# A two-layer convolution and MLP network with its gradients on one core: layer 1's forward in a fixed order on PE, and loads, stores and a normalisation moved within their queues

## The chip, the core and the metric

The kernel runs on one core of a Trainium2 chip. The metric is the device time of one execution in microseconds (us). Engines are named as in the profile: PE multiplies matrices (PEld is its weight load), DVE is the vector engine, ACT the scalar (activation) engine, POOL the general one, and SP issues most of the DMAs. [...]

## What is computed

The reference runs a forward pass of four blocks on 2048 tokens of 448 features, and returns its output together with the gradients of all inputs:

```python
x = A_q
x = x + A(layernorm(x), k, v, shift_k, ssm_k, ssm_D)   # q * (long convolution of kv + kv * D)
x = x + B(layernorm(x), w1, w2)                        # silu(x @ w1) @ w2, 448 -> 1792 -> 448
x = x + A(layernorm(x), k, v, shift_k, ssm_k, ssm_D)
x = x + B(layernorm(x), w1, w2)
out, vjp = jax.vjp(f, A_q, A_k, A_v, A_shift_k, A_ssm_k, A_ssm_D, B_w1, B_w2)
return (out, *vjp(grad_out))
```

Within A, k is convolved with a kernel of four taps (shift_k) and multiplied by v to give kv; kv is convolved along the sequence with ssm_k, by Fourier transforms of length 4096 in the reference; the result multiplies the layer's normalised input. The convolution's output Y doesn't depend on x, so both layers share it.

## The kernel before

**The prefix (`_ssm_prefix`).** It computes Y by a two-stage Fourier transform written as matmuls: `conv` makes kv from k by four-tap matmuls, `stage1_kv` and `_fft_stage1` the first stage, `turn` transposes on PE, `_fft_stage2` the second stage. The spectrum K of ssm_k stands in the tile Z (as Ka), and KB holds K with its halves swapped, which takes DMAs from SBUF to SBUF (`_swap_halves_dma`, shown as KB<-Z, issued by POOL). A loop of eight rounds (h, i) runs conv for kv, the first stage of the round before, the turns of K (first half) and the second stage of K (second half). In rounds 2 and 3 it also does the first layer normalisation of token group 0 (`_ln`, lines 425 and 426; tile na0, input x0c0), pinned in its place among DVE's and ACT's instructions. `cons_ka` copies K's chunks out of PSUM and stores them to DRAM (spec_K, line 413), and `cons_prod` does the same with the spectrum of kv (spec_KV, line 448), then multiplies it by Ka and by KB (pa, pb) for the inverse transform. Both kinds of store are issued by POOL, and so share its queue with the swaps. The weights w1sb and w2sb are asked for after the call of the prefix (lines 185 to 189), on SP.

**The layers (`Main`).** Tokens run in four chunks of 512 (c), each of four tiles of 128. `first` makes X, the normalised input and its transpose nT for chunk 0. `a_fwd` is block A for one chunk: normalisation, product with Y, sum into X. `b_pre` is block B's normalisation, `b_tr` the transposition to nT (`transp`: 2 x 8 transpositions on PE into ps_t, and two copies to nT). `h(c, L, nT, half, hold)` computes half of the 1792 hidden features in four groups of one or two tiles of 128: matmuls into ps_h (line 537, tag mm, two buffers), the silu to aT on ACT (L629), and a copy dT of the input to silu (L113), which the gradient needs. That copy is made by DVE, except for the third group of half 0, whose copy is ACT's. `out` multiplies aT by w2sb (ps_o, line 658, tag po with two buffers) and adds it to X on DVE (L659).

The 448 features of nT are three full blocks of 128 and one of 64 rows. `contract` orders a group's matmuls: `at` other than 0 puts the whole ones first and the half ones (64 rows) last, `at` 0 the other way round. [...]

In the first loop of `run`, chunk c of layer 1 does h for half 1, b_tr for chunk c+1, h for its half 0, and then `out` for chunk c. The order on each engine is the framework's choice from its own costs, with the order of the program as priority. The second loop does layer 2's forward together with layer 2's backward (`ga`: gradient of the hidden features, ps_g, ghp, ghT; `gn`: ps_n, line 740, and the backward of the normalisations), the third layer 1's backward with the weight gradients (`ps_d`, line 904) woven in.

**Spilled tiles.** aT and ghT are turned by DMA transposes (`store_turned`, L503; one buffer "turned") and stored to A_d and GH_d (L504) one step later by `flush`; the dT of layer 1 are stored to DT_d and loaded again (`load_d`, L769, tile dTl, tag D with three buffers). ACT turns dTl into silu's slope in place (`slope`, L614), in layer 1's backward in a hook after each tile's lb_u (L742). In `ga` the load for a later chunk and the turn of the present ghT come at the same step.

**The end (`_gw1`).** It computes the last weight gradient, feature tile by feature tile: two loads of 512 KB (dstat<-GH_d, L902, and dstat<-GP_d, L900, a DMA transpose), 32 matmuls, a copy dout on ACT; `turn` turns dout by a DMA transpose to do (L941), and `store` stores the tile turned before (L933, L934). These DMAs are all SP's.

Of the kernel before, what the change touches and what calls it, by code (L numbers as in the profile page):

```python
# [17 lines left out]
P = 128  # L18
S = 2048
D = 448  # L20
# [100 lines left out]
def kernel(  # L121
# [60 lines left out]
    k.yk = ctx.enter_context(tc.tile_pool(name="yk", bufs=1, side="right", reuse_waits="tile"))  # L182
    k.Ysb = k.yk.tile([P, J, D], BF16, name="Ysb", tag="Y")
    _ssm_prefix(k)
    k.w1sb = k.wk.tile([P, ND, F], BF16, name="w1sb", tag="WA")
    nc.sync.dma_start(out=k.w1sb[:, 0:3, :], in_=k.B_w1[0:384].rearrange("(c p) f -> p c f", p=P))
    nc.sync.dma_start(out=k.w1sb[:, 3, :], in_=k.B_w1[320:448])
    k.w2sb = k.wk.tile([P, NF, D], BF16, name="w2sb", tag="WB")
    nc.sync.dma_start(out=k.w2sb[:], in_=k.B_w2.rearrange("(c p) d -> p c d", p=P))
    k.psum = ctx.enter_context(tc.tile_pool(name="psum", bufs=1, space=PSUM, reuse_waits="tile"))  # L190
    k.xg = ctx.enter_context(tc.tile_pool(name="xg", bufs=1, side="right", reuse_waits="tile"))
    k.Xp = k.xg.tile([P, NT, 512], BF16, name="X", tag="X")
# [94 lines left out]
def _ssm_prefix(k):  # L287
# [4 lines left out]
    with ExitStack() as es:  # L292
# [113 lines left out]
        def cons_ka(ci, ps):  # L406
            sl = slice(ci * 1024, (ci + 1) * 1024)
            _copy(nc, bal.pick(1024), Ka[:, sl], ps[:])
            if ci % 2 == 1:
                lo, hi = (ci - 1) * 1024, (ci + 1) * 1024  # L410
                if ci > 8:
                    _swap_halves_dma(k, KB, Ka, lo, hi, nc.gpsimd)
                nc.gpsimd.dma_start(out=k.SPEC_d["K"][:, lo:hi], in_=Ka[:, lo:hi])

        k.na0 = k.dp.tile([P, 4, D], BF16, name="na0", tag="dstat", bufs=3)
        prev = None
        for h in range(2):
            for i, jq in enumerate((1, 2, 3, 0)):
                kvt = conv(h, jq)
                if prev:  # L420
                    stage1_kv(*prev)
                prev = (h, jq, kvt)
                if h == 0:
                    turn(A1Kf, Z, (0, 1, 5, 6)[i])
                if 4 * h + i in (2, 3):
                    _ln(k, work, 0, lambda tl: k.x0c0[:, tl, :], 0, k.na0, ((2 * i - 4, 2 * i - 2),), pin=True, store=i == 3)
                if h == 1:
                    _fft_stage2(k, Z, psum, cons_ka, range(2 * i, 2 * i + 2))
        for i in range(4):
            _swap_halves_dma(k, KB, Ka, 2048 * i, 2048 * (i + 1), nc.gpsimd)  # L430
        stage1_kv(*prev)
        A1f = A1kv[:].rearrange("p a c n s -> p a (c n s)")
        for i in range(3):
            _fft_stage2(k, Z, psum, cons_ka, range(8 + 2 * i, 10 + 2 * i))
# [8 lines left out]
        def cons_prod(ci, ps):  # L443
            sl = slice(ci * 1024, (ci + 1) * 1024)
            xs = Zf[:, sl]
            _copy(nc, bal.pick(1024), xs, ps[:])
            if ci % 2 == 1:
                nc.gpsimd.dma_start(out=k.SPEC_d["KV"][:, (ci - 1) * 1024:(ci + 1) * 1024], in_=Zf[:, (ci - 1) * 1024:(ci + 1) * 1024])
            pa = work.tile([P, 1024], BF16, name="pa", tag="pa", bufs=4)
            pb = work.tile([P, 1024], BF16, name="pb", tag="pb", bufs=4)  # L450
            nc.vector.tensor_tensor(out=pa[:], in0=xs, in1=Ka[:, sl], op=ALU.mult)  # L451
            nc.vector.tensor_tensor(out=pb[:], in0=xs, in1=KB[:, sl], op=ALU.mult)  # L452
            bal.add("dve", 1.4)
            hold.append((pa, pb, ci))
            if len(hold) > 2:
                pa, pb, cj = hold.pop(0)
                _fft_inv_stage2_chunk(k, pa, pb, False, B1, cj, psum)
# [22 lines left out]
class Main:  # L480
# [58 lines left out]
    def transp(self, src, dst):  # L539
        nc, k = self.nc, self.k  # L540
        blocks = [(0, 128), (128, 256), (256, 384), (320, 448)]
        rows = P
        for h in range(2):
            pt = k.psum.tile([P, 2, 512], BF16, name="ps_t", tag="tr", bufs=2)
            for u in range(2):
                lo, hi = blocks[2 * h + u]
                for tl in range(4):
                    nc.tensor.transpose(pt[:rows, u, tl * P:(tl + 1) * P], src[:, tl, lo:hi], k.ident[:])
            _copy(nc, k.bal.pick(1024, dve_ns=0.53), dst[:rows, 2 * h:2 * h + 2, :], pt[:rows])

    def first(self):
# [24 lines left out]
                keep(nc.vector.tensor_scalar(out=n_g[:, tl, :], in0=X[:, tl, :], scalar1=r[:, tl:tl + 1], scalar2=nmr[:, tl:tl + 1], op0=ALU.mult, op1=ALU.add))  # L576
        nc.gpsimd.dma_start(out=_pm(k.N_d[1][:])[:, 0:4, :], in_=n_g[:])
        nT = self.ch.tile([P, ND, 512], BF16, name="nT", tag="nT", bufs=2)
        pts = [k.psum.tile([P, 2, 512], BF16, name="ps_t", tag="tr", bufs=2) for _ in range(2)]
        for tl in range(4):  # L580
            for b, lo in enumerate((0, 128, 256, 320)):
                nc.tensor.transpose(pts[b // 2][:, b % 2, tl * P:(tl + 1) * P], n_g[:, tl, lo:lo + P], k.ident[:])
        nc.scalar.copy(nT[:, 0:2, :], pts[0][:])
        self.held = keep(nc.vector.tensor_copy(nT[:, 2:4, :], pts[1][:])).ins
        return nT
# [28 lines left out]
            self.k.last_slope = self.nc.scalar.activation(s, s, ACT.Derivative_silu)  # L614
            self.k.bal.add("act", 0.5 * n)

    def h(self, c, L, nT, half, hold, pre=None):
        nc, k = self.nc, self.k
        aT = self.td.tile([P, NF // 2, 512], BF16, name="aT", tag="T", bufs=3)
        dT = self.td.tile([P, NF // 2, 512], BF16, name="dT", tag="D", bufs=3)  # L620
        hold.append((aT, dT))
        d0 = pre() if pre else None
        for ft0, n, at in ((0, 2, 1), (2, 2, 0), (4, 2, 1), (6, 1, 1)) if half == 0 else ((7, 1, 1), (8, 2, 1), (10, 2, 0), (12, 2, 1)):
            ps = k.psum.tile([P, 2, 512], FP32, name="ps_h", tag="mm", bufs=2)
            self.contract(ps, self.w1sb, nT, ft0, n, at)
            o = ft0 - 7 * half
            a = aT[:, o:o + n, :]
            tm = dT[:, o:o + n, :]
            last = nc.scalar.activation(a, ps[:, 0:n, :], ACT.Silu)  # L629
            e = nc.scalar if o == 4 or (o, c, L, half) == (0, 0, 0, 0) else nc.vector  # L630
            _copy(nc, e, tm, ps[:, 0:n, :])
            k.bal.add("act", 0.52 * n)
            k.bal.add(*(("act", 0.52 * n) if e is nc.scalar else ("dve", 0.6 * n)))
        if L == 1:
            if half == 1:
                with self.tc.issue_after(last.ins):
# [10 lines left out]
                self.next_piece()  # L647
        if L == 1:
            self.store_turned(k.A_d[1], aT, c, half)
        return d0  # L650

    def out(self, c, aT, last):
        nc, k, X = self.nc, self.k, self.X
        for tl in range(4):
            t = 4 * c + tl
            po = k.psum.tile([P, 512], FP32, name="ps_o", tag="tr" if last and tl % 2 else "po", bufs=2)
            for ft in range(NF):
                nc.tensor.matmul(po[:, :D], lhsT=aT[ft // 7][0][:, ft % 7, tl * P:(tl + 1) * P], rhs=self.w2sb[:, ft, :], start=(ft == 0), stop=(ft == NF - 1))  # L658
            nc.vector.tensor_tensor(out=X[:, t, :], in0=X[:, t, :], in1=po[:, :D], op=ALU.add)  # L659
            k.bal.add("dve", 0.62)  # L660
        if last:
            nc.gpsimd.dma_start(out=_pm(k.outs[0][0])[:, 4 * c:4 * c + 4, :], in_=X[:, 4 * c:4 * c + 4, :])

    def g_load(self, c):
        gb = self.ch.tile([P, 4, 512], BF16, name="gb", tag="gb", bufs=2)
# [14 lines left out]
    def ga(self, c, L, gT, dT, mid=None, loads=(None, None)):  # L680
# [3 lines left out]
        for fp in range(NF // 2):  # L684
# [15 lines left out]
            if fp in (3, 6):  # L700
                hh = (fp - 3) // 3
                if loads[hh]:
                    ld.append(self.load_d(*loads[hh]))
                if L == 1 or hh == 0:
                    self.store_turned(k.GH_d[L], ghT[hh], c, hh)
                else:
                    self.flush()
                    self.store_plain(nc.sync, k.GP_d, ghT[hh], c, 0)
# [77 lines left out]
    def run(self):  # L786
# [6 lines left out]
        def hook(d):  # L793
# [2 lines left out]
                    self.slope(d, (tl,))  # L796
            return run

        self.h(0, 0, nT, 0, cur)
        for c in range(4):  # L800
            if c < 3:
                with self.tc.issue_after(self.held):
                    self.a_fwd(c + 1, 0, xs[c])
                nb = self.b_pre(c + 1, 1)
            else:
                gb = self.g_load(0)
                na, nb = self.a_fwd(0, 2, None), self.b_pre(0, 3)
            self.h(c, 0, nT, 1, cur)
            nT = self.b_tr(nb)
            fol = []  # L810
            self.h((c + 1) % 4, 0 if c < 3 else 1, nT, 0, fol)
            if c == 3:
                gT = self.g_turn(gb[:])
            self.out(c, cur, False)
            cur = fol
        for c in range(4):
            d0 = self.h(c, 1, nT, 1, cur, (lambda: self.load_d(0, 0)) if c == 3 else None)
            if c < 3:
                na1 = self.a_fwd(c + 1, 2, None)
            self.out(c, cur, True)  # L820
            if c < 3:
                gb_next = self.g_load(c + 1)
            if c == 3:
                with self.tc.issue_after(k.last_slope.ins):
                    self.slope(d0)
            box = []
            if c < 3:
                ghT = self.ga(c, 1, gT, cur, lambda fp: box.append(self.b_pre(c + 1, 3)) if fp == 2 else None)
# [14 lines left out]
            na, nb = na1, nb1  # L843
            if c < 3:
                gb = gb_next
        k.jobs = _gw2(k, k.dp, range(3), [(k.dp, "dstat", 3)], first=k.go_jobs.ins)
        bb = nc.cur_bb.bb

# [73 lines left out]
def _gw1(k, pool, slots):  # L922
# [13 lines left out]

    def turn(ft, o):
        if ft < NF - 2:
            store()
            o7 = pool.tile([P, ND, P], BF16, name="do7", tag="do7", bufs=2)  # L940
            nc.sync.dma_start_transpose(out=o7[:], in_=o[:])  # L941
            turned.append((ft, o7))
            return
        store()
# [278 lines left out]
```

## Time and profile before

| What | us |
|---|---|
| Median of three runs (737.02 to 741.23) | 739.4 |
| The profiled execution | 738.77 |
| Its span, from first to last instruction | 736.6 |
| Prefix and start of the layers, to the first ps_h | 0 to 102.5 |
| Layer 1's forward, to the first group of layer 2's chunk 0, half 1 | 102.5 to 211.6 |
| Layer 2's forward and backward | 211.6 to about 410 |
| Layer 1's backward | about 410 to 519.6 |
| Suffix (convolution's gradient, weight gradients) | 519.6 to 736.6 |
| PE busy 690.3, DVE 507.6, ACT 424.1, POOL 62.7 | share of span 94%, 69%, 58%, 9% |
| DMA: 180.11 MB, 245 GB/s as a mean | |

The busy time of PE is the union of its matmuls' times with modelled ends[...]. The stages overlap at their edges. In the window view each row is a stretch of the span with the busy time of each engine in it, the granted clock of PE and the mean share of the DMA engines; in the timeline a gap before an instruction stands in brackets with what ended it.

### The profile page before, as it was taken

What the parts mean: (1) busy time and instruction counts of PE and PEld (TensorE: products, weight loads), DVE (VectorE), ACT (ScalarE), POOL (GpSimd) and SP (SyncE); (2) the same over time, 40 slices, a digit from 0 to 9 for tenths busy, and PEclk for the clock granted to TensorE, in tenths of its full rate; (3) what the DMA queues carried; (4) which work ended last, traced back from release to release, by engine and by line L of the source; (5) the groups of instructions that cost most, each with busy time, mean ns of one, the idle gap of its engine ahead of it and who ended that gap; (6) DMA issues with size and microseconds to landing.
All of it is one profiled execution on the core that took longest, in us unless ns stands there. A gap on an engine that the chain in (4) does not pass through costs nothing. (4 is left out here: it accounts for less than half of the span.)

```text
span 736.6 us, 12192 instructions
## 1 busy us (share of the span) xinstructions
PE 690.3 (94%) x4753; PEld 362.6 (49%) x4753; DVE 507.6 (69%) x1059; ACT 424.1 (58%) x539; POOL 62.7 (9%) x111
## 2 busy tenths in 40 slices
PE   6988789999999998999999799999999999999987
PEld 5766533443344443443444334445465767755533
DVE  4878888787743597895958788798224777199423
ACT  4688877766437577487576476763723666531101
POOL 1143221111100002000000000000000000000000
PEclk9999999999999999999999989999999999999999
DMA  9979969999875878979999999997799999899966
GB/s 311 240 179 277 354 212 319 280 290 281 244 153 143 202 158 208 188 205 200 239 223 289 185 348 263 255 270 257 268 252 215 297 322 348 279 275 243 208 144 154
DMA packets 234789, 180.11 MB, mean 245 GB/s; under 512 B 179178, under 2 KB 215598, under 8 KB 233580
## 3 DMA queue, kind: packets, MB, share of 16 engines
q1 hardware_dynamic: 228238, 156.34, 82.4%
q0 software_dynamic: 5872, 22.65, 9.0%
q8 instruction: 37, 0.61, 0.4%
q10 hardware_dynamic: 622, 0.35, 0.3%
q14 instruction: 20, 0.16, 0.1%
HBM read 69.58 MB, written 63.77 MB: 181 GB/s over the span
## 5 line engine op out<-in xcount | busy, mean ns | idle before, releaser
L904 PEld LDWEIGHTS <-dstat 128*128 128x128 bf16 x896 | 85.1, 98 | 80.8 <-DMA dstat<-GP_d 4.4
L537 PE MATMUL ps_h<-nT,w1sb 128*128 128x512 bf16 (+1 forms) x448 | 102.1, 381 | 6.8 <-DVE dT L113 5.2
L537 PE MATMUL ps_g<-gT,w2T 128*128 128x512 bf16 (+1 forms) x448 | 96.0, 381 | 3.2 <-ACT ghp L690 3.1
L740 PE MATMUL ps_n<-w1T,ghT 128*128 128x448 bf16 x448 | 92.6, 360 | 5.0 <-ACT lb_u L742 3.6
L904 PE MATMUL ps_d<-mov,dstat 128*128 128x448 bf16 x448 | 89.5, 352 | 3.5 <-DMA dstat<-GP_d 3.5
L629 ACT ACTIVATE aT<-ps_h 128x1024 bf16<-128x1024 f32 (+1 forms) x64 | 58.4, 916 | 55.2 <-PE ps_h L537 38.3
L658 PE MATMUL ps_o<-w2sb,aT 128*128 128x448 bf16 x448 | 90.1, 353 | 0.0
L113 DVE CAST dT<-ps_h 128x1024 bf16<-128x1024 f32 (+1 forms) x55 | 58.3, 1063 | 27.8 <-ACT aT L629 27.8
L537 PEld LDWEIGHTS <-w1sb 128*128 128x128 bf16 (+1 forms) x448 | 35.9, 96 | 69.7 <-issue 41.2
L740 PEld LDWEIGHTS <-ghT 128*128 128x128 bf16 x448 | 43.5, 99 | 48.6 <-issue 7.7
L537 PEld LDWEIGHTS <-w2T 128*128 128x128 bf16 (+1 forms) x448 | 35.4, 96 | 61.9 <-issue 29.2
L690 ACT CAST ghp<-ps_g 128x1024 bf16<-128x1024 f32 x56 | 55.4, 1007 | 17.1 <-PE ps_g L537 13.1
L658 PEld LDWEIGHTS <-aT 128*128 128x128 bf16 x448 | 42.4, 98 | 42.3 <-issue 3.6
L904 PE MATMUL ps_d<-X,dstat 128*128 128x448 bf16 x224 | 52.2, 353 | 0.0
L904 PE MATMUL ps_d<-GO,dstat 128*128 128x448 bf16 x224 | 50.2, 353 | 0.0
L742 ACT ACTIVATE lb_u<-ps_n,rstd 128x448 f32<-128x448 f32 x32 | 20.2, 633 | 37.0 <-DVE X L727 17.7
L966 ACT CAST dout<-ps_d 128x448 bf16<-128x448 f32 x14 | 7.5, 534 | 51.8 <-PE ps_d L904 43.9
L233 PEld LDWEIGHTS <-pb 128*128 128x128 bf16 x336 | 32.5, 98 | 9.1 <-DVE pb L452 5.7
L614 ACT ACTIVATE dTl<-dTl 128x1024 bf16<-128x1024 bf16 (+1 forms) x32 | 29.8, 944 | 12.0 <-DMA dTl<-DT_d 12.0
L232 PEld LDWEIGHTS <-pa 128*128 128x128 bf16 x336 | 32.8, 98 | 7.2 <-DVE pa L451 4.3
L698 DVE TENSOR_TENSOR ghT<-dT,ghp 128x1024 bf16<-128x1024 bf16 (+1 forms) x32 | 19.8, 621 | 20.4 <-ACT ghp L690 20.3
L659 DVE TENSOR_TENSOR X<-X,ps_o 128x448 bf16<-128x448 bf16 x32 | 19.7, 615 | 16.3 <-PE ps_o L658 16.2
(188 smaller groups left out, 1091.7 us busy)
## 6 DMA issues: line engine op xcount, KB each, us to landing
A_d<-turned SPq DMA_DIRECT2D x12, 896.0 KB, 4.6
GH_d<-turned SPq DMA_DIRECT2D x12, 896.0 KB, 5.1
dstat<-A_d SPq DMA_DIRECT2D x21, 512.0 KB, 5.0
dstat<-GH_d SPq DMA_DIRECT2D x21, 512.0 KB, 4.7
DT_d<-dT SPq DMA_DIRECT2D x8, 896.0 KB, 6.5
dTl<-DT_d SPq DMA_DIRECT2D x8, 896.0 KB, 6.6
spec_K<-Z POOLq DMA_DIRECT2D x7, 512.0 KB, 7.5
KB<-Z POOLq DMA_DIRECT2D x14, 256.0 KB, 12.5
```

Of the source, the lines that this page charges most:

```text
L113: eng.tensor_copy(out, in_)
L232: nc.tensor.matmul(o, lhsT=pa[:, i * P:(i + 1) * P], rhs=k.Gsb[:, ga, :], start=True, stop=False)
L233: nc.tensor.matmul(o, lhsT=pb[:, i * P:(i + 1) * P], rhs=k.Gsb[:, gb, :], start=False, stop=True)
L537: self.nc.tensor.matmul(o, lhsT=w[lo:hi, b, f:f + P], rhs=r, start=(seen[u] == 1), stop=(seen[u] == ND))
L614: self.k.last_slope = self.nc.scalar.activation(s, s, ACT.Derivative_silu)
L629: last = nc.scalar.activation(a, ps[:, 0:n, :], ACT.Silu)
L658: nc.tensor.matmul(po[:, :D], lhsT=aT[ft // 7][0][:, ft % 7, tl * P:(tl + 1) * P], rhs=self.w2sb[:, ft, :], start=(ft == 0), stop=(ft == N ...
L690: k.last_gh = nc.scalar.copy(gh[:], ps[:])
L698: nc.vector.tensor_tensor(out=ghT[hh][:, o:o + len(u), :], in0=dT[hh][1][:, o:o + len(u), :], in1=gh[:, u[0]:u[0] + len(u), :], op=ALU.mult)
L740: mm = nc.tensor.matmul(pn[:, :D], lhsT=ghT[ft // 7][:, ft % 7, tl * P:(tl + 1) * P], rhs=self.w1T[:, ft, :], start=(ft == 0), stop=(ft == ...
L742: last_u = nc.scalar.activation(u0[:], pn[:, :D], ACT.Identity, scale=k.rstd[2 * L + 1][:, t:t + 1], accum_out=cp[:, tl, 0:1])
L904: i = k.nc.tensor.matmul(ps[:, :D], lhsT=st[:, t, :], rhs=mov[:, t, :], start=start and t == 0, stop=stop and t == NT - 1)
```

## The change

It has six parts.

1. Layer 1's forward runs in a fixed order on PE. `in_turn` wraps each group of h, each transposition half and each part of out so that its PE instructions stand behind the last one of the block before (`_in_turn`, which the suffix already uses, with `k.tail`). `h` becomes a generator `h_groups`, and `out` is split into `out_part`s, which stand between the groups.
2. In `contract`'s calls the positions of the half matmuls change, so that those of neighbouring groups join. This holds for both layers.
3. A chunk's a_fwd moves: the one for chunk c+2 stands after b_tr for chunk c+1 (`first_norm`).
4. In the prefix the first normalisation moves from rounds 2 and 3 to rounds 0 and 1; the stores of both spectra go from POOL to SP; the loads of the weights stand after the last `stage1_kv`.
5. In layer 1's backward the turn of ghT stands behind the load of dTl on SP.
6. In the last weight gradient a block is turned first and the one before it stored after that.

```diff
     _ssm_prefix(k)
-    k.w1sb = ...
...
-                nc.gpsimd.dma_start(out=k.SPEC_d["K"][:, lo:hi], in_=Ka[:, lo:hi])
+                nc.sync.dma_start(out=k.SPEC_d["K"][:, lo:hi], in_=Ka[:, lo:hi])
...
-                if 4 * h + i in (2, 3):
-                    _ln(k, work, 0, lambda tl: k.x0c0[:, tl, :], 0, k.na0, ((2 * i - 4, 2 * i - 2),), pin=True, store=i == 3)
+                if 4 * h + i in (0, 1):
+                    _ln(k, work, 0, lambda tl: k.x0c0[:, tl, :], 0, k.na0, ((2 * i, 2 * i + 2),), pin=True, store=i == 1)
...
         stage1_kv(*prev)
+        k.w1sb = k.wk.tile([P, ND, F], BF16, name="w1sb", tag="WA")
+        nc.sync.dma_start(out=k.w1sb[:, 0:3, :], in_=k.B_w1[0:384].rearrange("(c p) f -> p c f", p=P))
+        nc.sync.dma_start(out=k.w1sb[:, 3, :], in_=k.B_w1[320:448])
+        k.w2sb = k.wk.tile([P, NF, D], BF16, name="w2sb", tag="WB")
+        nc.sync.dma_start(out=k.w2sb[:], in_=k.B_w2.rearrange("(c p) d -> p c d", p=P))
...
-                nc.gpsimd.dma_start(out=k.SPEC_d["KV"][:, (ci - 1) * 1024:(ci + 1) * 1024], ...)
+                nc.sync.dma_start(out=k.SPEC_d["KV"][:, (ci - 1) * 1024:(ci + 1) * 1024], ...)
...
-        for ft0, n, at in ((0, 2, 1), (2, 2, 0), (4, 2, 1), (6, 1, 1)) if half == 0 else ((7, 1, 1), (8, 2, 1), (10, 2, 0), (12, 2, 1)):
+        for ft0, n, at in ((0, 2, 1), (2, 2, 0), (4, 2, 1), (6, 1, 0)) if half == 0 else ((7, 1, 1), (8, 2, 0), (10, 2, 1), (12, 2, 0)):
             ps = k.psum.tile([P, 2, 512], FP32, name="ps_h", tag="mm", bufs=2)
-            self.contract(ps, self.w1sb, nT, ft0, n, at)
+            with self.in_turn():
+                self.contract(ps, self.w1sb, nT, ft0, n, at)
...
+            yield
...
+    def in_turn(self):
+        return _in_turn(self.k) if self.fixed else ExitStack()
...
+    def out_part(self, c, aT, tl, lo, hi, po=None, tag="po"):
...
+        with self.in_turn():
+            for ft in range(lo, hi):
                 nc.tensor.matmul(po[:, :D], ...)
...
+                    with self.tc.issue_after(k.d_load.ins) if L == 0 and loads[hh] else ExitStack():
+                        self.store_turned(k.GH_d[L], ghT[hh], c, hh)
...
         self.h(0, 0, nT, 0, cur)
         for c in range(4):
+            if c == 0:
+                with self.tc.issue_after(self.held):
+                    na = first_norm(1)
+            if c == 3:
+                gb = self.g_load(0)
+            nb = self.b_pre((c + 1) % 4, 1 if c < 3 else 3)
+            g = self.h_groups(c, 0, nT, 1, cur)
+            next(g), next(g)
+            po = [self.out_part(c, cur, 0, 0, 7)]
+            list(g)
+            po.append(self.out_part(c, cur, 1, 0, 7))
+            for tl in range(2):
+                self.out_part(c, cur, tl, 7, NF, po[tl])
+            self.out_part(c, cur, 2, 0, NF)
+            nT = self.b_tr(nb)
             if c < 3:
+                na = first_norm(c + 2)
             fol = []
+            g = self.h_groups((c + 1) % 4, 0 if c < 3 else 1, nT, 0, fol)
+            next(g), next(g)
+            self.out_part(c, cur, 3, 0, NF)
+            list(g)
...
+        self.fixed = False
...
         if ft < NF - 2:
-            store()
             o7 = pool.tile([P, ND, P], BF16, name="do7", tag="do7", bufs=2)
-            nc.sync.dma_start_transpose(out=o7[:], in_=o[:])
+            with k.tc.issue_after(nc.sync.dma_start_transpose(out=o7[:], in_=o[:]).ins):
+                store()
             turned.append((ft, o7))
```

Each `next(g)` runs one group of h, and `list(g)` the rest with the stores of its tiles; `in_turn` ends with the first loop, after which the order on PE is free again.

## The prediction, made before the changed kernel was run

> **What bounds the kernel now.** I read the page first, then a table of stages by windows, then the PE timeline at each place where the table shows PE idle, and last the queue of SP, which issues most DMAs.
>
> ```profile
> span 736.6 us, 12192 instructions
> ...
> PE 690.3 (94%) x4753; PEld 362.6 (49%) x4753; DVE 507.6 (69%) x1059; ACT 424.1 (58%) x539; POOL 62.7 (9%) x111
> ```
>
> PE is the bound nearly everywhere; only its idle time, its slow clock and its mode changes can be won. Which stages hold them (columns: window, length, busy us of PE, PEld, DVE, ACT, POOL, clock, DMA share, GB/s):
>
> ```profile
> 38.00:46.00 8.00, 5.83 (x61) 5.06 (x59) 4.74 (x12) 6.42 (x11) 3.31 (x5) 0.79 0.77 102
> 84.00:99.00 15.00, 11.05 (x97) 6.67 (x97) 12.94 (x23) 10.03 (x13) 3.49 (x6) 1.00 1.01 382
> 160.00:187.00 27.00, 24.53 (x131) 10.71 (x129) 21.33 (x42) 16.28 (x22) 2.64 (x3) 1.00 1.14 288
> 418.00:429.00 11.00, 7.39 (x26) 3.04 (x24) 6.34 (x21) 5.70 (x9) 0.00 (x0) 0.69 1.22 194
> 520.00:700.00 180.00, 178.87 (x1591) 109.75 (x1591) 100.97 (x170) 80.57 (x93) 4.71 (x12) 1.00 0.98 273
> 700.00:716.00 16.00, 12.48 (x65) 5.89 (x64) 2.28 (x4) 1.06 (x2) 1.46 (x4) 1.00 0.60 129
> ```
>
> Idle PE and a clock below 1 stand in the same rows twice. From 520 to 700 nothing is idle, so time won earlier reaches the end in full. The two places on PE, timeline (start, length, what, idle before):
>
> ```profile
> 39.17 1.03 PE L221 MATMUL ps_s<-Z,Gsb 128*128 128x512 bf16 x4
> 42.37 2.97 PE L383 MATMUL ps_cv<-KB 112*128 112x112 bf16 x32 [2.17 <-ACT A1kv L111]
> ...
> 422.95 5.38 PE L740 MATMUL ps_n<-w1T,ghT 128*128 128x448 bf16 x14 [3.61 <-ACT lb_u L742]
> ```
>
> The same 32 convolution matmuls take 1.74 us at 36.83, and the 8 of L399 after them 0.93 at 38.41 but 1.37 at 45.13; the same 14 of L740 take 2.81 at 416.15: after each idle stretch work runs at about half speed. Why ACT was late at 422.95 stands in SP's queue, and so does the idle time at 706 to 716:
>
> ```profile
> 405.42 0.37 SPq L504 DMA_DIRECT2D GH_d<-turned  x1
> 410.37 2.83 SPq L503 DMA_TRANSPOSE turned<-ghT  x1
> 413.24 0.58 SPq L769 DMA_DIRECT2D dTl<-DT_d  x1
> ...
> 705.99 1.21 SPq L941 DMA_TRANSPOSE do<-dout  x1
> 710.30 0.39 SPq L933 DMA_DIRECT2D out_dram<-do  x1
> 711.29 2.52 SPq L900 DMA_TRANSPOSE dstat<-GP_d  x1
> ```
>
> The load of the derivatives (L769) stands behind a turn that waits 4.5 us for its buffer; ACT's slope waits for that load until 421.2. At 705.99 a turned block is issued, its store waits for the landing (4.2 us), and the GP_d load behind it reaches PE at 715.97.
>
> [...] Here a change between whole and half contractions costs 310 ns start to start instead of 216. [...]
>
> **The change part by part.** The sum is against the profiled execution, 738.77 us, 2.17 more than its span; the median shown is 739.4, so I add 0.6 at the end.
>
> *First normalisation, rounds 2 and 3 to 0 and 1.* It is 4 statistics (0.62 us), 4 aggregations (0.18) and some small ones on DVE, about 3.6 us, and 4 x 0.75 = 3.0 us on ACT. Now these fall at 35.8 to 44.5, and PE idles 2.17; then the clock costs 2.97-1.74 = 1.23 and 1.37-0.93 = 0.44. Sum 3.84. Rounds 0 and 1 (26 to 33) have ACT gaps of 1.3, 1.8 and 1.0 us and DVE gaps of 1.0, 0.8 and 1.1; its input landed at 24.0. DVE lacks about 0.7 us there, so I expect at most 0.6 of new PE idle: -3.2 (bounds -3.8, and +1 if ACT's copies queue behind the norm's wait for POOL's power, 1.0 us).
>
> *Spectra from POOL to SP.* Fourteen stores of 512 KB leave POOL (0.53 to 0.57 us each, and waits for earlier landings); the swaps KB<-Z behind them go earlier. Today the last four are issued between 69.5 and 75.5 and land 83.3 to 87.5; DVE waits 1.76 us for one at 84.75, and PE 1.56. On SP they wait for the copies of ACT and DVE; w1sb and w2sb, now issued at 54 to 57, are moved ahead of the later spectra by the diff, and x0c (needed at 102, landed 97 to 101) stands behind the last. The bytes are the same with DMA full, so I take -1.3 (bounds -1.9 and +1.5, x0c late).
>
> *Layer 1's forward in fixed order.* Prices from starts on PE: 512 columns 216 ns, 448 columns 190, a transposition 56, a pair of halves 216, each change of mode 95 more. One chunk is 14 x 3.5 x 0.216 = 10.6 for L537, 56 x 0.190 = 10.6 for L658, 0.9 for 16 transpositions, and with the pairs joined 4 runs of halves x 0.19 = 0.8: 23.0 with nothing waiting. Today a chunk (from one first group of half 1 to the next: 110.38, 134.08, 159.56, 186.25, 211.58) takes 23.7, 25.5, 26.7, 25.3, in all 101.2; matmuls of L658 fill in, and casts behind statistics still make PE wait (0.75, 1.06, 0.45 at 162 to 178). The fixed order has waits of its own, worked out from these rows:
>
> ```profile
> L629 ACT ACTIVATE aT<-ps_h 128x1024 bf16<-128x1024 f32 x48 | 48.9, 1021 | 36.9 <-PE ps_h L537 34.8 <-issue 1.5 <-ACT na L278 0.6
> ...
> L113 DVE CAST dT<-ps_h 128x1024 bf16<-128x1024 f32 x39 | 47.5, 1220 | 21.5 <-ACT aT L629 21.5
> ...
> L111 ACT COPY nT<-ps_t 128x1024 bf16<-128x1024 bf16 x14 | 13.6, 1011 | 0.0
> ```
>
> After the transpositions the next group needs both nT copies, both on ACT now, and nothing stands between: 0.7 for the first, 0.5 for the second. Groups 4-5, 6, 7, 8-9 follow each other with two buffers: the third needs ACT's silu and copy of the first (0.09+0.92+1.01 = 2.0 us after its end at 1.8, so 3.85 against 2.6): 1.3; the fourth waits 0.3 for the cast of the second. So 23.0+2.8 = 25.8 a chunk, 103.2 for four; the first block (5.8 plus three such waits, 7.7) is as now (7.9). That is +2. Behind these waiting matmuls stands all of PE. In exchange the norm of chunk c+2 moves half a chunk ahead of the one it collided with, which I count in bringing today's DVE waits to none. If casts still stand behind four statistics (3.1 us) it costs up to +3 a chunk; if the copies and silus come earlier than I reckon, -1 a chunk. I take +2.
>
> *Paired halves in layer 2,* order free: one run of halves fewer in each of 8 half chunks, 8 x 0.19 = 1.5, of which fillers may break half: -0.8 (bounds -1.5, +0.5).
>
> *Derivative inputs ahead of the turned block.* The slot of the load comes free when DVE ends at 407.5. Issued then and landing in the usual 6.6 us, it is there at 414.1; ACT's slope ends at 415.2, lb_u of the second tile runs at 416.3, and PE's fourth tile finds its buffer. Gone are 3.61 of idle and 5.38-2.81 = 2.57 of clock, 6.2. What is late next is DVE: a tile costs it 5.2 us (tile 1 from 418.5 instead of 422.9), so I give back 1.2: -5.0 (bounds -6.2, -1). Two transposes of chunk 1 move behind its load, from 434.4 to about 440, and delay x_turn (needed at 481) and GH_d (needed late), which nobody feels; a later load at 450.8 slipping by 4 us would cost ACT about 1.
>
> *Turned blocks of the last gradient.* The store of the previous block goes after the next turn and finds it landed; SP no longer stops for 4.2 us each 6 us, and GP_d loads come earlier. Gone: 1.36+2.16 = 3.52 at 706 to 716. SP still issues 1.2+0.9+2.5+0.5 = 5.1 us per 6.1: -3.0 (bounds -3.5, 0).
>
> Sum: -3.2-1.3+2.0-0.8-5.0-3.0 = -11.3: 727.5, or 728.1 beside the median.
>
> **Rivals.** *A, the fixed order pays:* the trace has DVE waits inside the blocks that an even load would remove; with 24.2 a chunk it is -4.4 in place of +2: 721.7. Against it: no filler where nT is copied. *B, the moved transfers were hidden or are replaced:* the slope load still lands late behind GH_d and dstat (8.0 us was seen) and the prefix stays DMA-bound: derivative -1.5, first norm -2, spectra 0, tail -3, layer 1 +2, layer 2 -0.8: 734.1. *C, slower:* in the fixed order of layer 1 casts stand behind statistics in both halves of each chunk with no filler. Price 2 x 3.1 us for each of 4 chunks, +25, less the 13.3 won elsewhere and with the +2 counted: 739.4+27-13.3 = 753. It decides from 3.3 us a chunk above today's 25.3; DVE is busy 21.3 of 27 us in the window above, which speaks for it; that the statistics need nothing of the groups beside them, and can run early, against.
>
> **How the numbers follow.** Main case 0.46, A 0.20, B 0.19, C 0.15. The range from 720 to 739 leaves out C and some of A. A change below 0.5% (3.7 us) can't be told from none by a measurement of this kernel. Faster than 735.7: nearly all of main and A, and two thirds of B, 0.74; within 0.5%: the rest, 0.11; slower 0.15. The main case's own range is 722 to 734.
>
> **What would show it.** Clock 1.0 at 38 to 46 and no idle of 2 us; swaps landed before 80; PE idle before the group after the transpositions and before half 1's first group in each chunk, and chunks near 25.8; clock 1.0 and no lb_u stall after the first ps_n of layer 1's backward; no GP_d wait over 0.5 at the end. I am wrong if chunks take over 28 us, if the slope still waits over 3 us for dTl, or if the idle near 40 only moves to 30.

## The result, and the profile after

The changed kernel takes 743.87 us (median of 15, 738.98 to 749.65) beside 739.4 for the kernel before in the same comparison (15 runs, 734.38 to 741.23): ratio 1.0077, interval 1.005 to 1.0104. It became 0.8% slower, where 728.1 was predicted. The profiled executions (738.77 and 747.27 us) lie further apart than the medians, by 8.5 us against 4.5. What follows reads these single executions; the ratios of the medians check it in the experiments. The span went from 736.6 to 745.5 us, and PE is busy for 3 us more:

```profile
span 745.5 us, 12197 instructions
...
PE 693.4 (93%) x4753; PEld 363.5 (49%) x4753; DVE 508.3 (68%) x1059; ACT 424.8 (57%) x539; POOL 55.1 (7%) x97
```

The same number of matmuls (4753) being busy for longer points to a slower clock somewhere. Windows show where (columns: window, length, busy us of PE, PEld, DVE, ACT, POOL, clock, DMA share, GB/s; the first row answers to the first of before; the next five are layer 1's first block and its four chunks, each from one first group of half 1 to the next):

```profile
38.00:46.00 8.00, 7.54 (x109) 6.83 (x109) 5.07 (x8) 6.69 (x12) 2.06 (x3) 1.00 0.48 160
100.40:109.60 9.20, 8.42 (x28) 2.54 (x28) 5.82 (x15) 5.12 (x6) 1.62 (x2) 0.71 0.23 66
109.60:140.20 30.60, 24.57 (x131) 10.82 (x129) 23.56 (x55) 18.98 (x26) 5.88 (x7) 1.00 0.99 273
140.20:171.40 31.20, 26.65 (x129) 11.01 (x129) 21.99 (x45) 17.29 (x23) 3.39 (x5) 0.89 0.76 214
171.40:200.20 28.80, 25.62 (x128) 11.16 (x128) 19.96 (x44) 15.11 (x20) 4.42 (x5) 0.94 0.95 228
200.20:226.10 25.90, 24.80 (x134) 11.29 (x134) 10.00 (x11) 10.06 (x12) 0.00 (x0) 1.00 0.83 218
```

Three chunks take 28.8 to 31.2 us, with idle PE of 3 to 6 us and a clock below 1 in two of them. The fourth, in which DVE and ACT have half as much to do, because it has no normalisation beside it, takes 25.9. In the kernel before the four chunks take 23.7 to 26.7 us, all at full clock; the second of them:

```profile
134.10:159.60 25.50, 24.35 (x130) 10.69 (x129) 19.67 (x44) 18.48 (x25) 5.58 (x7) 1.00 1.09 294
```

To follow the time through the whole kernel I take the start on PE of a few first instructions; between them, in us:

| stretch on PE | before | after | difference | predicted |
|---|---|---|---|---|
| up to the first convolution (inputs) | 24.40 | 25.17 | +0.8 | 0 |
| from there to the first group of layer 1 | 78.12 | 75.26 | -2.9 | -4.5 |
| to layer 2's first gradient group (layer 1) | 126.03 | 141.71 | +15.7 | +2.0 |
| to the first matmul of ps_sk | 459.50 | 458.98 | -0.5 | -5.8 |
| to the end of the span (turned blocks) | 48.59 | 44.37 | -4.2 | -3.0 |

The differences add up to 8.9 us, the whole of the span's. The first row is not the change's: over all traces it lies between 24.2 and 28.3 us. Layer 1's row carries the loss. Adding PE's gaps over 0.15 us within layer 1 gives 15.3 us after and 5.4 before: 6.2 of them end with ACT's copy of nT, 5.4 with ACT's cast of dT, 3.7 with DVE's cast. Without its gaps the row is 126.5 us after and 120.6 before, 5.9 more. Slow clock is more than that: the rows above with 0.71, 0.89 and 0.94 lose 2.7, 3.4 and 1.7 us by their length times what the clock lacks, 7.8 in all. Some 2 us come back, as it seems from the joined halves (in experiment 11, nearly the same order at full clock, the row without gaps is 118.1). And the 2.7 us of the first block are not the fixed order's: in experiment 1, with the old order, the stretch loses 2.7 us there too (clock 0.57 from 102.2 to 108.5). That leaves about 13 of the 15.7 us for the fixed order. The two largest gaps, PE timeline of the changed kernel:

```profile
133.97 2.92 PE L537 MATMUL ps_h<-nT,w1sb 128*128 128x512 bf16 x12 [0.26 <-DVE dT L113]
140.16 2.40 PE L537 MATMUL ps_h<-nT,w1sb 128*128 128x512 bf16 x6 [3.27 <-ACT dT L111]
...
159.80 0.59 PE L537 MATMUL ps_h<-nT,w1sb 128*128 128x512 bf16 x2 [2.94 <-ACT nT L111]
160.71 4.39 PE L537 MATMUL ps_h<-nT,w1sb 128*128 128x512 bf16 x14 [0.32 <-ACT nT L111]
```

What ACT and DVE did ahead of 140.16, their timelines:

```profile
133.92 1.40 ACT L273 ACTIVATE nb<-X,ln_nmr,rstd 128x448 bf16<-128x448 bf16 x2
137.54 0.76 ACT L273 ACTIVATE na<-x0c,ln_nmr,rstd 128x448 bf16<-128x448 bf16 x1 [2.22 <-issue]
138.21 1.00 ACT L641 ACTIVATE aT<-ps_h 128x1024 bf16<-128x1024 f32 x1
139.11 1.00 ACT L111 CAST dT<-ps_h 128x1024 bf16<-128x1024 f32 x1
```

```profile
134.50 1.21 DVE L113 CAST dT<-ps_h 128x1024 bf16<-128x1024 f32 x1
135.62 0.17 DVE L262 BATCH_NORM_AGGREGATE ln_mv<-ln_st 128x2 f32<-128x6 f32 x1
135.83 0.17 DVE L264 TENSOR_SCALAR ln_ve<-ln_mv 128x4 f32<-128x4 f32 x1
...
137.29 0.16 DVE L268 SCALAR_TENSOR_TENSOR ln_nmr<-ln_mv,rstd 128x4 f32<-128x4 f32 x1 [0.77 <-POOL rstd L266]
```

Group 4-5 was done on PE at 135.75, and its silu could have run then. But a scaling (na, L273) stood ahead of it in ACT's queue, and that needs ln_nmr, which DVE makes at 137.29 from POOL's power (L266), which waited for ln_ve at 135.83, which stood on DVE behind a cast. ACT stood still for 2.22 us with a silu ready behind it; silu and cast then end at 140.1, and only then has group 7 a buffer. At 156.9 the same happens with the nT copies: a scaling waits until 158.09 with both copies behind it. After both gaps PE runs at about half speed: six matmuls of 512 columns take 2.40 us in place of 1.46.

What the prediction looked for elsewhere came as follows. At 38 to 46 the clock is 1.0, but PE now idles 1.19 us at 35.71 (for ks on ACT) and 0.74 at 38.19 (for Z on DVE). In layer 1's backward no lb_u stall is left, but at 521.27 PE waits 2.97 us for the weight-gradient block dstat<-A_d. No GP_d wait is left at the end.

### The profile page after: what moved, and what is told of

It is laid out like the page before. It is cut to its first block, busy times and chain, and to the rows that moved or that the text cites. A ratio compares the mean times of both kernels' runs of the same rounds, so it can differ in the third digit from the quotient of the medians.

```text
span 745.5 us, 12197 instructions
## 1 busy us (share of the span) xinstructions
PE 693.4 (93%) x4753; PEld 363.5 (49%) x4753; DVE 508.3 (68%) x1059; ACT 424.8 (57%) x539; POOL 55.1 (7%) x97
## 5 line engine op out<-in xcount | busy, mean ns | idle before, releaser
L537 PE MATMUL ps_h<-nT,w1sb 64*128 64x512 bf16 (+1 forms) x448 | 107.5, 400 | 18.0 <-ACT nT L111 6.2
L671 PE MATMUL ps_o<-w2sb,aT 128*128 128x448 bf16 x448 | 89.6, 354 | 0.1
L537 PEld LDWEIGHTS <-w1sb 64*128 64x128 bf16 (+1 forms) x448 | 35.7, 99 | 84.8 <-issue 58.8
L759 PEld LDWEIGHTS <-ghT 128*128 128x128 bf16 x448 | 43.5, 99 | 45.4 <-DVE ghT L716 4.3
L671 PEld LDWEIGHTS <-aT 128*128 128x128 bf16 x448 | 43.6, 98 | 43.3 <-issue 2.7
L228 PE MATMUL ps_v<-Gs,pb 128*128 128x128 bf16 x224 | 28.0, 219 | 0.1
```

The lines of the kernel that those rows point to most:

```text
L228: nc.tensor.matmul(o, lhsT=pb[:, i * P:(i + 1) * P], rhs=k.Gsb[:, gb, :], start=False, stop=True)
L537: self.nc.tensor.matmul(o, lhsT=w[lo:hi, b, f:f + P], rhs=r, start=(seen[u] == 1), stop=(seen[u] == ND))
L759: mm = nc.tensor.matmul(pn[:, :D], lhsT=ghT[ft // 7][:, ft % 7, tl * P:(tl + 1) * P], rhs=self.w1T[:, ft, :], start=(ft == 0), stop=(ft == ...
```

## The experiments

The theory after the first reading: the fixed order lets waits of ACT and DVE through to PE, because a normalisation that waits for another engine stands in their queues ahead of silus, casts and copies. Rivals: the moved parts are worth less than they seem; the new order of the groups costs by itself; DVE's statistics are too much work at the wrong place. "Stretch" below is layer 1 as in the table (126.0 before, 141.7 after), and all ratios are to the kernel before.

**1. Layer 1 put back, everything else kept.** All of `run`, `h`, `out`, `transp` and `first` as before:

```diff
+        self.h(c, 0, nT, 1, cur)
+        nT = self.b_tr(nb)
...
+        self.out(c, cur, False)
```

> The changed kernel with layer 1's forward, its groups and its order as in the kernel before; the first normalisation, spectra, derivative load and turned blocks stay moved. Theory (the fixed order of layer 1 costs about 15 us, the moved parts gain about 6.5 as the trace of the changed kernel has it: 2.1 ahead of layer 1 and 4.5 behind it): about 730 us, ratio to before 0.991. Rival (the moved parts are worth nothing or cost something, and the trace's gain behind layer 1 comes from the paired halves): 737 to 740.

729.6 us, ratio 0.9902 (0.9883 to 0.992). The moved parts gain nearly 1% and the loss is layer 1's: by the ratios (1.0077 less 0.9902, times 739.4 us) it is 12.9 us, about as the trace had it. This reckoning, here and below, leaves some 3 us open either way.

**2. PE's order free, the new emission kept.**

```diff
-        k.tail, self.fixed = None, True
+        k.tail, self.fixed = None, False
```

> The changed kernel with its own emission of layer 1, but PE's order free again. Theory (what costs is that PE may not pass a group whose ACT copy is late): the scheduler fills the waits with matmuls of L671, layer 1 takes about 109 us as before, and the time is 730. Rival (the new emission, with the norm of chunk c+2 half a chunk earlier and the parts of ps_o, costs by itself): layer 1 stays near 120 us and the time above 738.

731.6 us, ratio 0.9923 (0.9903 to 0.9943); stretch 126.5. The halves' pairing, the parts of ps_o and the earlier norm cost nothing that can be told from none beside experiment 1; fixing PE's order does, 11.4 us by the ratios.

**3. Scalings on DVE.**

```diff
-        _ln(k, self.ch, c, src, si, n_g)
+        _ln(k, self.ch, c, src, si, n_g, eng=nc.vector if self.fixed else None)
```

(and the same in `b_pre`.)

> The changed kernel with the normalisations of layer 1's forward multiplied out on DVE in place of ACT, order fixed as in the change. Theory (ACT's queue stands at a normalisation that waits for the power on POOL, with silu, cast and the copy of nT behind it): the waits of 3.3 and 2.9 us at 136.5 and 156.9 go, chunks 1 to 3 fall from 30 to about 26, the time falls by 10 to 12 us to about 733. Rival (DVE's statistics ahead of its casts are what costs): DVE gets 28 x 0.39 = 11 us more, its casts come later still, and the time stays at 743 or rises.

745.4 us, ratio 1.0098 (1.0072 to 1.0123); stretch 140.8. This is a miss for the theory as it stood. ACT's waits fall from 11.6 to 7.3 us, but waits for DVE's casts rise from 3.7 to 8.1, one of 3.88 us one group later, between groups 7 and 8-9. The cast that frees the buffer there stands on DVE behind ln_nmr, which waits 1.16 us for POOL, and behind the scalings (1.31 us), the product and the sum (1.09 us each). So moving the scaling to the other queue doesn't help; the round trip and the added work (DVE is busy for 96.9 us of the stretch in place of 87.8), which the rival named, both stand ahead of the cast, and this run doesn't part them.

**4. Only the prefix, on the kernel before.** First normalisation and spectra moved, with the loads of the weights.

```diff
-                if 4 * h + i in (2, 3):
+                if 4 * h + i in (0, 1):
...
-                nc.gpsimd.dma_start(out=k.SPEC_d["K"][:, lo:hi], in_=Ka[:, lo:hi])
+                nc.sync.dma_start(out=k.SPEC_d["K"][:, lo:hi], in_=Ka[:, lo:hi])
```

> The kernel before with only the first normalisation and the spectra moved. As the trace of the changed kernel has it: 2 us of gain, 737. As predicted: 4.5 us, 735. Rival: the gain ahead of layer 1 is given back in layer 1's first chunks, since x0c lands later: 739.4 or more.

733.5 us, ratio 0.9951 (0.9934 to 0.9968), -3.0 us from first convolution to first group in the trace: as the changed kernel's trace had it (-2.9).

**5. Normalisations held behind casts, order fixed.** Each `next(g)` gives the group's cast.

```diff
+            with self.tc.issue_after(next(g)):
+                nb = self.b_pre((c + 1) % 4, 1 if c < 3 else 3)
...
+            *_, cast = g
+            if c < 3:
+                with self.tc.issue_after(cast):
+                    na = first_norm(c + 2)
```

> The changed kernel, order on PE still fixed, with the two normalisations of a chunk held behind casts: that of chunk c+1's second half behind the cast of the second group of half 1, that of chunk c+2 behind the last cast of half 1, so that both fall beside the 35 matmuls of L671 in place of the four groups in a row. Theory (the fixed order itself is sound, 24.9 us a chunk where no statistics stand in the row of groups; what costs is where DVE's and ACT's norm work stands in their queues): chunks 25 to 27 us, layer 1 about 106 to 109, time about 728 to 731. Rival (a fixed order with two buffers for ps_h and no filler costs by itself, whatever stands beside it): waits move, chunks stay at 29 to 31, time above 740.

748.0 us, ratio 1.0122 (1.0091 to 1.0152); stretch 144.6. The wait between groups 6 and 7 is now 1.05 us in every later chunk, as in the changed kernel's last ones; but two others grew. PE and ACT timelines of this kernel:

```profile
149.74 2.81 PE L671 MATMUL ps_o<-w2sb,aT 128*128 128x448 bf16 x14 [1.71 <-DVE X L673]
...
155.47 0.59 PE L537 MATMUL ps_h<-nT,w1sb 128*128 128x512 bf16 x2 [2.03 <-ACT nT L111]
156.38 4.37 PE L537 MATMUL ps_h<-nT,w1sb 128*128 128x512 bf16 x14 [0.32 <-ACT nT L111]
```

```profile
146.89 2.71 ACT L273 ACTIVATE nb<-X,ln_nmr,rstd 128x448 bf16<-128x448 bf16 x4 [1.78 <-DVE ln_nmr L268]
151.82 2.71 ACT L273 ACTIVATE na<-x0c,ln_nmr,rstd 128x448 bf16<-128x448 bf16 x4 [2.21 <-DVE ln_nmr L268]
154.44 1.89 ACT L111 COPY nT<-ps_t 128x1024 bf16<-128x1024 bf16 x2
```

The norm of chunk c+2 now makes ACT wait 2.21 us right before the nT copies, and DVE's addition to X (which frees the buffer of ps_o) runs only at 149.10, behind the four statistics of that norm (from 146.77 on). The wait can be moved by hand, but a fixed order lets it through where it lands. That the order is sound once statistics are out of the row is refuted.

**6. Statistics left out** (stats is false in layer 1's forward; two small copies of four columns stand in for them).

```diff
-        for tl in range(lo, hi):
+        for tl in range(lo, hi) if stats else ():
```

> The changed kernel with the mean and variance of layer 1's normalisations left out (32 + 11 bn_stats and their aggregations; the power, the scaling and all else stay), to measure what their place in the queues costs. Theory: all four chunks like the last one, near 25 us, layer 1 about 107 to 109 against 125, time about 728. Rival (waits for copies and for the power on POOL): chunks 28 or more, time above 738.

740.5 us, ratio 1.0025 (1.0005 to 1.0045); stretch 139.7. A clear miss. The trace has 32 statistics and 32 aggregations fewer (not 43, as I had expected), DVE is busy for 71.7 us of the stretch in place of 87.8, and only 2.0 us of it go; by the ratios (1.0025 against 1.0077) it is 3.8 us of the whole. A gap of 3.85 us is still there at 143.63, with the same order on ACT ahead of it: a scaling that starts at 141.01 after POOL's power, and the silu of group 4-5 behind it at 141.68. So the busy time of the statistics is the smaller part of what costs.

**7. Only the derivative load moved, on the kernel before.**

```diff
+                    with self.tc.issue_after(k.d_load.ins) if L == 0 and loads[hh] else ExitStack():
+                        self.store_turned(k.GH_d[L], ghT[hh], c, hh)
```

> The kernel before with only the derivative load issued ahead of the turned block. As predicted: 5.0 us of gain, ratio 0.993. As the traces now have it (the stall at the load is 3.6 us in one execution of the order of before and 1.2 in another, and a wait of 1 to 3 us for a weight-gradient block comes later in three of the kernels with the load moved): about 1.5 us, ratio 0.998.

738.3 us, ratio 0.9983 (0.9954 to 1.0012): no gain that can be told from none. The stall of 3.61 us is gone, and one of 3.28 us for dstat<-A_d stands at 508.58; from layer 2's first gradient group to ps_sk it is 458.3 us, 1.2 below before. Nor was the stall always so long: in experiments 4 and 8, with the load in its old place, the same stretch takes 457.1 and 456.8 us, and the stall is 1.17 and 1.49 us there, and the fourteen matmuls after it take 2.81 us in both (5.38 behind the stall of before). Over all traces this stretch takes 456.8 to 459.5 us with the load in its old place (three traces) and 454.3 to 459.3 with it moved in every chunk (ten).

**8. Only spectra and weights moved, on the kernel before.** Experiment 4 without the normalisation:

```diff
-                if 4 * h + i in (0, 1):
+                if 4 * h + i in (2, 3):
```

> The kernel before with only the spectra on SP and the weights ahead of them. Of the 2.9 us that both moves ahead of layer 1 gave, as predicted 1.3 are the spectra's: ratio 0.998. Rival (the idle time near 40 only moved to rounds 2 and 3, and the gain is the swaps'): 2 to 3 us, ratio 0.996.

736.3 us, ratio 0.9969 (0.9949 to 0.9989). From first convolution to first group 75.82 us, 2.3 below before. Not all of that is the spectra's. Experiment 7 has the prefix of before, and the clock stays full after the same wait of 2.2 us (from 43.00 there to Z's matmuls at 46.18 it is 3.18 us, against 3.17 in this run, whose clock is 1.00 from 42.3 to 46.0, and 3.96 before); its stretch is 77.42 us. So of the 3.0 us of experiment 4, 0.7 are the clock that the profiled execution of before had lost, 1.6 the spectra's (with the weights) and 0.7 the first normalisation's.

**9. The round trip left out.** In place of statistics, power and product, constants; the scalings stay:

```diff
+        else:
+            nc.gpsimd.memset(r[:, lo:hi], 1.0)
+            r = nmr = k.mhalf
```

> The changed kernel with layer 1's normalisations cut to their scaling: mean, variance, power and the product of both are left out, and the scaling takes constants, so that ACT waits neither for DVE's statistics nor for POOL's power. Leaving out the statistics alone took 2 us from layer 1 (139.7 against 141.7 from its first group to layer 2's first gradient group). Theory (the round trip DVE, POOL, DVE, ACT stands in queues ahead of silu and casts, and a fixed order shows it as PE's waits, with slow clock after each): without it that stretch takes about 127 us and the time is about 731. Rival (the row of four groups over two buffers and the nT copies are what costs): the stretch stays above 136 and the time above 739.

732.6 us, ratio 0.994 (0.9916 to 0.9964); stretch 130.3, so 11.4 of the 15.7 us are gone where the statistics alone had given 2.0: 4.2 are gaps (15.3 to 11.1) and 7.2 clock, of which 1.4 stand in the first block. By the ratios 10.1 us are gone. PE timeline of this kernel, a chunk and a bit:

```profile
161.29 3.02 PE L542 MATMUL ps_h<-nT,w1sb 128*128 128x512 bf16 x11 [1.05 <-ACT dT L111]
...
177.62 0.38 PE L542 MATMUL ps_h<-nT,w1sb 128*128 128x512 bf16 x1 [0.65 <-ACT nT L111]
178.53 2.96 PE L542 MATMUL ps_h<-nT,w1sb 128*128 128x512 bf16 x14 [0.54 <-ACT nT L111]
...
187.78 2.37 PE L542 MATMUL ps_h<-nT,w1sb 128*128 128x512 bf16 x9 [1.05 <-ACT dT L111]
```

From 161.29 to 187.78 it is 26.5 us, and the waits left are the ones that the prediction worked out, a little shorter: 0.65 and 0.54 for the copies, 1.05 and 0.39 (at 167.64) in the row. That is the fixed order without a norm in its way.

**10. L671 free, groups and transpositions fixed.**

```diff
-        with self.in_turn():
+        with ExitStack():
             for ft in range(lo, hi):
                 nc.tensor.matmul(po[:, :D], ...)
```

> The changed kernel with the groups and transpositions of layer 1 still in the change's order, but the matmuls of L671 free to go between them. Theory (what the fixed order takes away is the filler in the waits): layer 1 as with a free order, the stretch about 127 us, the time about 731. Rival (the order of the groups itself costs): above 738.

730.4 us, ratio 0.9905 (0.9871 to 0.994); stretch 126.5, 15.2 less than in the changed kernel (12.7 us less by the ratios). With all norms, statistics and powers in place, nothing is lost once the matmuls of L671 may go between the groups. PE's longest gap in the stretch is 1.2 us, and the clock is 1.00 all through.

**11. One filler placed by hand, order fixed.**

```diff
-            self.out_part(c, cur, 3, 0, NF)
-            list(g)
+            po = self.out_part(c, cur, 3, 0, 7)
+            list(g)
+            self.out_part(c, cur, 3, 7, NF, po)
```

> The changed kernel with the last seven of the fourteen matmuls of the fourth output tile moved by hand between group 6 and group 7, so that the row of four groups is broken by 1.35 us of work, order still fixed. Theory (round trip of the norm, 3 to 4 us where it falls on the row): the wait of 1.05 us that each chunk has without norms goes, 4 us at most, time about 739 to 741. Rival (it is only the missing filler in this one place): chunks at 25, the stretch about 128, time about 731.

734.6 us, ratio 0.9973 (0.9953 to 0.9993); stretch 130.5. More than my theory gave it: seven matmuls at another place (1.35 us a chunk) take 11.2 us from the stretch. Only 2.9 of these are gaps (15.3 to 12.4; those for ACT's cast fall from 5.4 to 0.9). The other 8.4 are mostly clock, 2.7 of them in the first block: no gap is over 1.6 us now, and the window from 103 to 230 has a clock of 1.00. By the ratios it is 7.7 us. I had left the clock out of this expectation.

**12. Experiment 10 with the load moved in one chunk only.**

```diff
-                    with self.tc.issue_after(k.d_load.ins) if L == 0 and loads[hh] else ExitStack():
+                    with self.tc.issue_after(k.d_load.ins) if L == 0 and c == 0 and loads[hh] else ExitStack():
```

> The changed kernel with L671 free (as in the run before) and the derivative load ahead of the turned block only in the first chunk of layer 1's backward, where the stall of 3.6 us was; in the later chunks the turned block goes first again. Theory (the weight-gradient block A_d, which PE awaits for 1 to 3.6 us near 507 in most kernels with the load moved, is late because later loads push the turned blocks and with them SP's queue back): the wait near 507 goes, 727 to 728. Rival (the block lands when it did before, at 506, whatever the order of the loads, and PE comes earlier): the wait stays at 2 to 4 us, time 730.

729.1 us, ratio 0.9893 (0.9863 to 0.9923), span 727.1: the lowest of all these kernels, 1.1% below the one before. The wait near 507 is gone. In experiment 10 it read

```profile
506.35 0.93 PE L941 MATMUL ps_d<-GO,dstat 128*128 128x448 bf16 x4 [3.60 <-DMA dstat<-A_d]
507.12 4.50 PE L759 MATMUL ps_n<-w1T,ghT 128*128 128x448 bf16 x14
```

and at the same work here

```profile
503.46 0.92 PE L941 MATMUL ps_d<-GO,dstat 128*128 128x448 bf16 x4
504.22 2.81 PE L759 MATMUL ps_n<-w1T,ghT 128*128 128x448 bf16 x14
```

The block landed at 506.3 there and at 501.0 here: the load that it needs was issued at 497.9 and at 492.9, behind turned blocks; that later derivative loads had pushed these back is argued, not shown. Experiment 9, with the load moved in every chunk, has no such wait either: counted from layer 2's first gradient group, the block lands at 274.2 us there, at 274.4 here and at 279.2 in experiment 10. By the ratios experiments 1, 10 and 12 can't be told apart; the spans are 729.2, 730.5 and 727.1.

## Why the prediction was wrong, point by point

**Layer 1, the step that failed.** The sum gave 23.0 us of work and 2.8 of waits, 25.8 a chunk, and the chunk without a norm beside it takes 25.9 (with 0.65 + 0.32 of waits for nT; in the row six matmuls of layer 2 fill the place of the wait at 224.92). In experiment 9 two chunks take 25.9 and 26.5. So the chunk without norms was priced well. What failed is the next sentence, where the norm of chunk c+2 moving half a chunk ahead "I count in bringing today's DVE waits to none", at +2 in all. A norm is not a block of work that can be laid elsewhere. It is a path through DVE (statistics), POOL (1.03 us of power), DVE (ln_nmr), ACT (four scalings of 0.75) and back to DVE, and silus, casts and copies stand among its steps in the queues of DVE and ACT. In the trace a step that waited stopped the ones behind it: the silu that could have run at 135.75 ran at 138.21, behind the scaling that waited 2.22 us, and the two nT copies ran at 158.76, behind one that began at 158.09. In the kernel before these stops are there too (ACT waits 4.61 us for ln_nmr ahead of 135.21, with two silus behind the scalings), but PE has matmuls of L671 (L658 there) to put in (22 of them from 129.91, and PE is busy for 8.45 of the 9 us from 130 to 139). The fixed order took that away: three chunks at 28.8 to 31.2, and +15.7 us, or 13 without the first block's clock, in place of +2. The runs bear this out from three sides. Without the first block's clock, cutting the round trip gives 10.0 us back (9), filler at one place 8.6 (11), and free filler all, 12.5 (10); by the ratios it is 10.1, 7.7 and 12.7. These are not parts of a sum: each also ends slow clock, and the clock was more than half of what 9 and 11 got back. In pricing waits of a chunk I had counted none of it.

**The bound on that step.** I gave it "+3 a chunk" if casts stood behind four statistics, and rival C, with two such waits a chunk, made 753 of that. C had the right place (a row of groups without filler) and the right sign, but for the most part the wrong mechanism: leaving the statistics out gave 2.0 us in the trace and 3.8 by the ratios (6). ACT, which my sum took to be free apart from its silus and copies, stood still for a product it needed. I had read DVE's waits in the trace before and not asked what ACT's own queue waits for.

**Spectra** gave 1.6 us in place of 1.3, within the bound of 1.9, and in the way that was told: the last swap lands at 79.3 in place of 87.5, and PE's wait of 1.56 us behind it is gone. **First normalisation** gave about 0.7 in place of 3.2. The prediction named this in its last lines ("only moves to 30"): the 2.17 us at 42.37 are gone, and 1.19 + 0.74 + 0.28 come at 35.7 to 43.5, because ks on ACT now stands behind the norm. I had allowed 0.6 for it. The 1.67 us that I had counted for the clock cost the profiled execution 0.7: at full clock, in experiment 7, PE reaches the next wait for ACT sooner (0.68 us for Z at 46.18). And they are lost in some executions and not in others (below).

**Derivative inputs.** The stall went, as predicted, with its clock (1.00 from 395 to 442); but in nine of the ten traces with the load moved in every chunk PE then waits 0.8 to 3.6 us for a weight-gradient block. No gain is shown (7) in place of 5.0, and the bound was "-1". I had gone through what else the moved transposes delay, and said that nobody feels it. As it seems, a load of dstat further down the same queue does: counted from layer 2's first gradient group it lands at 276.0 to 280.1 us in these nine traces and at 274.8 to 277.6 in the three of the old order, but at 274.2 in experiment 9. And 5.0 was read from one execution, whose stall and clock (6.2 us) were longer than in two others with the same order. Moved only in the one chunk that needs it, the load meets no such wait (12: 456.2 us from layer 2's first gradient group to ps_sk, 0.6 to 3.4 below the traces of the old order); that is one trace.

**Turned blocks:** -4.2 against the profiled execution of before, -3.0 predicted; this row is 44.3 to 44.4 us in all traces with the new order and 47.1 to 49.4 in the four with the old. **Paired halves in layer 2:** from its first gradient group to that of layer 1 it is 167.0 us after and 167.1 before, nothing in place of 0.8. In the trace of the changed kernel, in layer 1, the two halves of a pair start 3 ns apart (205.797 and 205.800), the pair of the next group follows 226 ns later, and the steps from whole to half and back take 312 and 309 ns from start to start, where it is 216 between whole ones.

Not settled: what makes the load of dstat late in most kernels with the derivative load moved; and in experiment 6, how much the changed positions of single DVE instructions add to what was left out, since the first chunk there waits longer than in the changed kernel and the later ones less.

## What to carry to other kernels

Before fixing an order on the engine that bounds, list for each wait it may no longer fill which queue the awaited instruction stands in, and whether anything ahead of it there waits for a third engine; here that round trip, more than the busy time, was what the fixed order showed. A safe middle way is to fix the order of the groups that must be in turn and to leave the matmuls that can wait free. And when a transfer is moved forward, follow the queue to the next load that something will wait for: what is gained at one stall can be given back there.

## What the runs showed of the hardware that had not been expected

In these traces the length of PE's idle time alone did not tell whether its clock fell after it. In the kernel before, 2.17 us of idle at 42.37 were followed by a clock of 0.54 from 42.3 to 46.0, and the 32 matmuls took 2.97 us. In experiment 8 the same wait at the same place was followed by full speed (1.00 from 42.3 to 46.0); its PE timeline:

```profile
42.38 1.73 PE L378 MATMUL ps_cv<-KB 112*128 112x112 bf16 x32 [2.17 <-ACT A1kv L111]
```

In the same way 3.60 us of idle ahead of 506.35 in experiment 10 were followed by a clock of 0.70 (506.3 to 512), and the fourteen matmuls of ps_n took 4.50 us; 3.28 us ahead of 508.58 in experiment 7 were followed by 1.00 (508.5 to 514), and the same fourteen took 2.81, as they did after 3.18 us in experiment 2. And a shorter wait, 2.03 us ahead of 155.47 in experiment 5, was followed by 0.72 (155 to 161). Three gaps of 1.43, 0.27 and 0.9 to 1.0 us stand ahead of layer 1 in the kernels of the table and of experiments 1 and 4; after them the first sixteen matmuls take 5.95 us in experiment 1 (clock 0.57 from 102.2 to 108.5) and 3.39 in experiment 4 (1.00 from 97 to 108).

No run was made to test what decides between the two. A price for slow clock behind a stall of 2 to 3.6 us, read from one execution, holds for that execution: experiments 2, 7 and 8 lost nothing behind waits of 2.17 to 3.28 us.
